# One core, an attention block with memory and an MLP: another hand-over order of the jobs, and the PSUM banks that go with it

## Chip, core and metric

One NeuronCore of a Trainium2 chip runs the whole program. The metric is the device time of one execution in microseconds. The kernel before takes 713.09 us, the median of three runs (712.26 to 713.43).

## What is computed

```python
x = A_x                                   # [1, 2048, 512]
xn = _layernorm(x)
return x + _A_ref(xn, wq, wk, wv, wo, beta) + _B_ref(xn, w1, b1, w2, b2)

def _A_ref(...):                          # 32 heads of 16, 4 segments of 512 tokens
    for s in range(4):
        logits = einsum("bhqd,bhkd->bhqk", qs, ks) * scale + mask
        a_dot = softmax(logits) @ vs
        a_mem = (phi(qs) @ M) / (phi(qs) @ z + 1e-6)
        outs.append(g * a_mem + (1 - g) * a_dot)
        M = M + phi(ks).T @ vs;  z = z + sum(phi(ks))
    return concat(outs) @ wo

def _B_ref(...):                          # 512 -> 1792 -> 512
    y = _layernorm(x)
    return gelu(y @ w1 + b1) @ w2 + b2
```

`phi(t)` is `t + 1` above zero and `exp(t)` below; `g = sigmoid(beta)`.

## The kernel before

Work is cut into **jobs**, a few instructions each. Attention has 16 units: unit i is segment i // 4 and a group of eight heads. The MLP has 16 half blocks: half block j is 256 tokens and half of the 1792 hidden columns. Most products are made of f16 high and low parts, three matmuls for one (`split3`, L465).

The jobs that the prediction speaks of, by the first word of their key, with the lines of their instructions:

- T: projection of queries or keys of a unit, 12 matmuls (L465, `xnT` with `wqs` or `wks`). ACT and DVE take the result out of PSUM (L481 to L495), SP stores it in DRAM (L486 to L488, `qd` or `kd`) and reads it back in another layout (L491, `qst` or `kst`). Scores of the unit can start only after that round trip.
- M: scores for the row maxima (L590, on PE) and the maxima on DVE (L597). R: one transpose (L605) and a second round trip of the maxima (L610, L613).
- S: scores the other way round (L630), exponentials on ACT (L635), masking on POOL (L644). pv and PV: probabilities times values (L659). O: the division (L507 to L513, L689 to L695).
- N, K, Z, Qd, Q: the memory part (L501, L569, L538, L543 to L550).
- V: values (L465). out: the output projection (L783).
- X, Xt, Y, Yt: normalization and transposes of the tokens (L450).
- D: one of the 7 hidden tiles of a half block, 12 matmuls of 256 columns (L465, `yT` with `w1s`), taken out by ACT or DVE (L724, L726). G: gelu (L731). H: the f16 split on POOL and ACT (L738 to L740). e: one of 14 parts of the second MLP product, six matmuls (L764).
- wl, wm, wf, ws: load, square sum, scale and f16 split of the weights, at the start.
- warm: eight matmuls on a tile of ones, whose result nobody reads (L796). There are 14 such jobs.

TensorE works in three **tilings**, which the trace shows as rows*columns of the array: the full array, 128*128 (T, V, D, out, N, transposes, warm); two tiles of 64 rows, on which two matmuls run side by side (M, S, e, Qd; shown as 48\*128, 50\*128 and 64\*128 after the rows in use); and four tiles of 32 columns, 128*32 (pv, K, R).

The order of all 1335 jobs is one string, `ORDER`. Each letter names one of 28 streams, and `plan()` takes the next job of that stream. A job hands its instructions to all engines at once, so the string sets the order on PE, ACT, DVE, POOL and SP, and each engine keeps it. A second string, `BANKS`, gives for every PSUM tile that a job takes (`dense()`) one of eight banks. A matmul that takes a bank waits until the last reader of the bank's previous tile is done.

Of the kernel before, what the change touches and what calls it, by code (L numbers as in the profile page):

```python
# [57 lines left out]
def streams():  # L58
# [43 lines left out]


ORDER = (
    "aacttuttcacutvaatcvucuevaatevaacvccvutbcbwtccvtbvvcwfvwtdcvttxxextxvwyxbchxgxxyxoowxoyxowowvyoyzoyzniiibccyygpz"
    "iiccniipznzyiyfzAnsqpiioiqizzmAqqiwpAzhoAoiiqqzzjpocjiqijjqizjoAjoBAiikskkAkjqiqjqmjjisqjiojiqbiskkkpkibbplafoA"
    "oAjpgjloojqjqjqjlohakkkpkojiqiAajsoijijqjiqjmiAiAifippBkkqqBikipqikoqilBsgaoplahqjjqlqqqjqjoBoijqiajqipamkkkksa"
    "ioojpiqjqiqijqjiaaqjqjsbmqiqBiiBfoikkkbBpkbibpghopoolqqpjqojjjloojiqjqiqilmkpkkkijojiqqqijjqijqiqjqiipkkkpkbiif"
    "mnillnglnnrjjrjqiirpjiqjisqijqikkmkkjijrjjioijioijikkpkkhilmfolomjjbgojqqjpljqjoobsmbkkkkjqqisjqqjijqiqjiqijoiq"
    "iiskkmippqiqpiskaklmiohlfoiqpqaqamqgploooaomjqjqqjqmjqaojpqpsiiqiqoioiqjpqiqiikkkkoapjiqijqijqjpqiqjqsjaqaoihkk"  # L110
    "kkaalmoqjjlbfobqjqjlsqmjgbbqjkkmmkkjqjqmojjjohiojiikkkkipiifplilonnliiiniipmripgnojjmjrjsjorijibkkkpkmiiqjqjqij"
    "qqiijsqiqjohjqiiqpqiipmkpkkskrillfmmlogqqbjjoojqjqjjoomkkpkkiijhooiqjiqjqijqiqpsjiqqjibbpqiqipkkkkliiqaslfoioom"
    "papqqqamgpooasjqqjqjmaoojqjlqjqiqiapqikmkikkiqipoiqjqjaoohijqjaqiqiisopaojiqqjiakmspkkklbopfjqlbqjmjgqjjqqjqlob"
    "bkkkmkmjqjqqiqjqijqjqoimijkpkkkliilfnimiiplgnniipirmoiorponijpjobojjioisjqqjpiiqkkkkiiprijsqsqjiqqjjimqqijrijkk"
    "ipkbsklfloqjqmjglojjqqqjjomsokkkkopjmioiijojqijqipqjqjqiiqqiikppkkkliqlfbbqliqqqimoipmgooojpjqqjojjoomjiikkkpki"
    "qijqijqjqiijqjiqjqiikisqpiskkkqpioqplooplqjjqqjjojjqlopkkkkjqjqqjjojqjoqqpspqkkkkqpqqlqqpqqmpqqqqqqqqqqqmqllqqr"
    "rrr"
)

BANKS = (
    "012345670123456174052316753401627354106237540612375406123754016237516237516237516231756237153672153675213675213"
    "675213765726132567132567132561723516725314607314607314067430167340176340167430167430164301643701643016743021543"
    "021435140235143021542301540123540125340125340152340152403156274031562740351640351640531640513645013465016354016"
    "354016354016354016534016534160543154602731452670315426073154206734215063741253741065370265237065237062537056237"
    "052635270635270652706523706532741534271354274135271435271435271435217406357214035610431054613054613054613054630"
    "546135045061345067123450673152046731520467315204637152046371520463715204637120543670512437065172065210765027106"
    "257106257106257106275062701652704136572043162045731625371627513627153627153627153627513267521376503476547036543"
    "706543765403765403765437403765403765403746052416052461052104621054621056421056241602543176032154760321547603215"  # L130
    "746032157460321576403215764302157642157641572647215762415274627154761245671267456741253607412536401720513674203"
    "764230764230764230764230764203726403752614037512640735124065214502615401256405126405164052164052164051264703512"
    "64351263451263470"
)


# [743 lines left out]
```

## Time and profile before

| | us |
|---|---|
| median of three runs | 713.09 |
| the profiled execution | 712.69 |
| its span, first to last instruction | 711.0 |
| PE busy | 693.3 |
| ACT busy | 535.9 |
| DVE busy | 531.8 |
| POOL busy | 363.7 |

A busy PE in this table is one that has a matmul in flight. A matmul of 512 columns is shown with about 380 ns, though in a row they start 216 ns apart, so the speed of PE has to be read from where groups start, not from their length. In the timeline a row's first number is the start of its group, and the start of the next row says how long the group held PE.

### The profile page before, as it was taken

The page shows a single profiled execution, that of the slowest core. Times are in us where ns is not written, and L with a number is a line of the kernel's source. Part 1 is how long each engine was busy: PE and PEld are TensorE (multiplying, and loading weights), DVE is VectorE, ACT ScalarE, POOL GpSimd, SP SyncE. Part 2 cuts the span into 40 slices and gives each one's busy share as a digit, 9 for nine tenths or more (in the row PEclk, how much of TensorE's full clock was granted, in tenths as well). Part 3 has the DMA queues.
Part 4 walks back from the last instruction along what each step waited for, and adds up shares of the span by engine and source line. Part 5 has one row for each costly group of instructions (what it writes and reads, how often), then busy time and mean ns, then how long its engine had stood idle before and what let it go on. Part 6 is the DMA issues. An engine that isn't in the chain of part 4 may idle for free.

```text
span 711.0 us, 16718 instructions
## 1 busy us (share of the span) xinstructions
PE 693.3 (98%) x6261; PEld 392.6 (55%) x6261; DVE 531.8 (75%) x1665; ACT 535.9 (75%) x934; POOL 363.7 (51%) x548
## 2 busy tenths in 40 slices
PE   7799999999999999999999999999999999999997
PEld 5464556565654565656554656566545545565542
DVE  5889867979684968978686786979688567978243
ACT  6897898868884678586975777687794768778960
POOL 4675758565632354555624446464724455455652
PEclk9999999999999999999999999999999999999999
DMA  9885233232303124131311412340413215031001
GB/s 288 236 247 152 61 71 96 62 90 74 95 4 103 60 70 113 48 96 42 92 43 57 111 47 77 96 115 2 115 24 103 78 20 146 15 93 19 1 17 59
DMA packets 54093, 59.30 MB, mean 83 GB/s; under 512 B 5038, under 2 KB 40892, under 8 KB 54012
## 3 DMA queue, kind: packets, MB, share of 16 engines
q1 hardware_dynamic: 51708, 54.04, 26.5%
q0 software_dynamic: 2304, 4.20, 3.8%
q8 instruction: 49, 0.80, 0.5%
q14 instruction: 32, 0.26, 0.1%
HBM read 41.18 MB, written 17.04 MB: 82 GB/s over the span
## 4 chain that ended last, share of the span: by engine, by line
PE 67%; DVE 12%; ACT 8%; DMA 6%; POOL 4%; issue 3%; SPq 1%; POOLq 0%; DVEq 0%; ACTq 0%
PE ps L465 26%; PE ps L764 14%; PE ps L659 8%; PE ps L783 6%; PE ps L630 4%; PE ps L590 4%; DVE ps L597 4%; ACT pt L635 3%; DMA kd<-hl 2%; PE ps L450 2%; PE ps L538 1%; DVE hl L485 1%; DMA w1s<-in_B_w_dram 1%; DVE mc L597 1%; DMA pt<-in_A_wv_dram 1%
## 5 line engine op out<-in xcount | busy, mean ns | idle before, releaser
L597 DVE CUSTOM_DVE_ANT_0 ps<-ps,mask 128x512 f32<-128x512 f32 (+3 forms) x512 | 235.0, 524 | 24.1 <-PE ps L590 23.2
L635 ACT ACTIVATE pt<-ps,qkcs 128x512 f32<-128x512 f32 (+1 forms) x384 | 206.9, 628 | 20.2 <-PE ps L630 17.7
L764 PE MATMUL ps<-w2s,hT 64*128 64x512 f16 x1344 | 176.2, 376 | 0.3 <-DVE fence L767 0.2
L465 PE MATMUL ps<-yT,w1s 128*128 128x256 f16 x1344 | 161.2, 273 | 2.5 <-DVE phk L495 1.2
L644 POOL TENSOR_SCALAR_AFFINE_SELECT pt<-pt 128x256 f32<-128x256 f32 x256 | 101.6, 419 | 110.1 <-ACT pt L635 109.2
L465 PEld LDWEIGHTS <-w1s 128*128 128x128 f16 x1344 | 127.2, 98 | 37.4 <-issue 16.9
L764 PEld LDWEIGHTS <-hT 64*128 64x128 f16 x1344 | 70.0, 94 | 57.4 <-issue 9.6
L740 POOL TENSOR_TENSOR hT<-hh,hT 128x512 f16<-128x512 f32 x64 | 66.5, 1039 | 66.7 <-ACT hT L739 65.5
L659 PE MATMUL ps<-pt,vt 128*32 128x512 f32 (+3 forms) x1024 | 77.6, 436 | 0.1
L597 DVE DVE_READ_ACCUMULATOR2_ANT mc<- 128x1 f32 x512 | 72.6, 142 | 0.2
L630 PE MATMUL ps<-qst,kst 50*128 50x512 f16 (+3 forms) x512 | 70.6, 298 | 0.1
L590 PE MATMUL ps<-kst,qst 48*128 48x512 f16 (+3 forms) x512 | 67.2, 298 | 0.7 <-DVE hT L726 0.4
L739 ACT ACTIVATE hT<-hh 128x512 f16<-128x512 f32 x64 | 36.7, 574 | 37.4 <-POOL hh L738 37.2
L738 POOL TENSOR_SCALAR hh<-hT,sc 128x512 f32<-128x512 f32 x64 | 42.6, 666 | 38.5 <-ACT hT L731 37.1
L659 PEld LDWEIGHTS ps<-pt,vt 128*32 128x32 f32 x1024 | 30.6, 109 | 42.0 <-issue 31.4
L724 ACT ACTIVATE hT<-ps,b1t,sc 128x256 f32<-128x256 f32 x64 | 36.6, 571 | 17.1 <-PE ps L465 16.6
L465 PE MATMUL ps<-xnT,wqs 128*128 128x512 f16 x192 | 45.0, 384 | 0.4 <-DVE mc L597 0.4
L783 PE MATMUL ps<-wos,oT 128*128 128x512 f16 x192 | 44.0, 380 | 0.9 <-POOL oT L695 0.6
L465 PE MATMUL ps<-xnT,wks 128*128 128x512 f16 x192 | 44.2, 380 | 0.0
L465 PE MATMUL ps<-wvs,xnT 128*128 128x512 f16 x192 | 43.5, 379 | 0.6 <-DVE hT L726 0.3
L726 DVE TENSOR_SCALAR hT<-ps,sc,b1t 128x256 f32<-128x256 f32 x48 | 25.7, 539 | 24.5 <-PE ps L465 24.4
L590 PEld LDWEIGHTS <-qst 48*128 48x128 f16 x512 | 27.1, 94 | 30.7 <-issue 14.8
(217 smaller groups left out, 958.7 us busy)
## 6 DMA issues: line engine op xcount, KB each, us to landing
xt<-in_A_x_dram SPq DMA_DIRECT2D x30, 256.0 KB
kd<-hl SPq DMA_DIRECT2D x48, 128.0 KB
kst<-kd SPq DMA_DIRECT2D x32, 192.0 KB
qd<-hl SPq DMA_DIRECT2D x48, 128.0 KB
qst<-qd SPq DMA_DIRECT2D x32, 192.0 KB
acc<-in_A_x_dram SPq DMA_DIRECT2D x16, 256.0 KB
acc<-in_B_b_dram POOLq DMA_DIRECT2D x16, 256.0 KB, 4.3
out_dram<-acc SPq DMA_DIRECT2D x16, 256.0 KB
```

Source lines behind the costliest of these rows:

```text
L465: T.matmul(p, wsl(ws, k, a), xsl(xs, k, b), start=s0 and i == 0, stop=s1 and i == 3 * n - 1)
L590: T.matmul(p[:, o:o + n], stk[i, 0][r, t, P * qb:P * qb + P], stk[i, 1][r, t, :n], start=True, stop=True)
L597: V.tensor_tensor_reduce(p[:, o:o + n], p[:, o:o + n], mask[:, 512 - n:], 1.0, -3e38, OP.add, OP.max, mc[i][:, 4 * b + t, qb:qb + 1])
L630: T.matmul(p[:, o:o + n], stk[i, 1][r, t, P * kb:P * kb + P], stk[i, 0][r, t, P * kb:], start=True, stop=True)
L635: A.activation(e[:, OFF[kbs[0]]:OFF[kbs[0]] + o], p[:, :o], AF.Exp, scale=qkcs[:, 1, i % NG:i % NG + 1])
L644: G.affine_select(v, v, pattern=[[0, 2], [1, P]], compare_op=OP.is_ge, fill=0.0, base=0, channel_multiplier=-1)
L659: T.matmul(p[32 * c:32 * c + 32, P * kb:], vt[s, kb][:, 4 * g + c, 16 * odd:16 * odd + 32], pt[i, 2 * c + odd][:, OFF[kb]:OFF[kb] + LEN[kb ...
L738: G.tensor_scalar(t, hz[:, z, :], col(SHH + j % 2), 0.0, op0=OP.mult, op1=OP.add)
L739: A.activation(hT[:, z, 0, :], t, AF.Copy)
L740: G.tensor_tensor(hT[:, z, 1, :], t, hT[:, z, 0, :], op=OP.subtract)
L764: T.matmul(pes[j][a], hTs[fh][r, fi, u, P * a:P * a + P], w2s[r, fo, v, :], start=n == 0 and m == 0, stop=fi == FH - 1 and m == 2, skip_gr ...
L783: T.matmul(p, o[:, u, P * b:P * b + P], wos[:, g, v, :], start=i == 0, stop=i == 3 * NG - 1)
```

## The change

The strings `ORDER` and `BANKS` are replaced by others of the same length, `ORDER` by the same letters in another order. No line of code is changed, and every engine runs the same computing instructions; only the waits between them are placed anew.

```diff
 ORDER = (
-    "aacttuttcacutvaatcvucuevaatevaacvccvutbcbwtccvtbvvcwfvwtdcvttxxextxvwyxbchxgxxyxoowxoyxowowvyoyzoyzniiibccyygpz"
+    "aacuccteauacvcacccttttutaatvaebvcbcuvvvttwdvabwccuvftvvvxctbvtwxwwxgeyxcyxxwwxxghoxoyoxccxoozyiiiozoiiyypzzpnii"
...
 BANKS = (
-    "012345670123456174052316753401627354106237540612375406123754016237516237516237516231756237153672153675213675213"
+    "012345670123456170324561732504617253046172530461725306172453061742061742016742016742017642017642016741260471264"
...
```

The following places show it. First PE, where the first MLP product of half block 9 (L465 with `w1s`, a full-array job) stands among scores of unit 9 (L630) and the memory update (L569). Each L465 row with another number of `ps` is one job D; rows that repeat are left out. Before:

```order
L630 LDWEIGHTS kst1_92
L630 MATMUL ps5_6279<-qst1_90,kst1_92 128x256
L630 MATMUL ps2_6280<-qst1_90,kst1_92 128x256
L465 LDWEIGHTS w1s_103
L465 MATMUL ps7_6287<-yT_5160,w1s_103 128x256
L465 MATMUL ps0_6301<-yT_5160,w1s_103 128x256
L569 MATMUL ps4_6315<-vt0_85,pkn_5973 32x48 x4
```

Now:

```order
L630 LDWEIGHTS kst1_92
L630 MATMUL ps2_6266<-qst1_90,kst1_92 128x384
L630 MATMUL ps1_6267<-qst1_90,kst1_92 128x384
L465 LDWEIGHTS w1s_103
L465 MATMUL ps7_6282<-yT_5099,w1s_103 128x256
L465 MATMUL ps0_6296<-yT_5099,w1s_103 128x256
L465 MATMUL ps5_6310<-yT_5099,w1s_103 128x256
L450 MATMUL ps3_6325<-ident_74,xt_5302 128x128 x4
L450 MATMUL ps6_6332<-ident_74,xt_5304 128x128 x4
```

Three jobs D and two transposes, all full-array jobs, stand in a row where two stood.

Second, PE again, where the scores of unit 14 begin (L590 with `kst0` and `qst0`), just behind the last job D of half block 13. Before:

```order
L465 LDWEIGHTS w1s_103
L465 MATMUL ps6_8732<-yT_7591,w1s_103 128x256
L630 LDWEIGHTS kst1_92
L630 MATMUL ps0_8752<-qst1_90,kst1_92 128x512
L630 MATMUL ps7_8753<-qst1_90,kst1_92 128x512
L590 LDWEIGHTS qst0_89
L590 MATMUL ps4_8764<-kst0_91,qst0_89 128x512
L590 MATMUL ps1_8765<-kst0_91,qst0_89 128x512
```

Now:

```order
L465 LDWEIGHTS w1s_103
L465 MATMUL ps0_8731<-yT_7560,w1s_103 128x256
L796 LDWEIGHTS ones_79
L796 MATMUL ps7_8745<-ones_79 128x256
L590 LDWEIGHTS qst0_89
L590 MATMUL ps5_8760<-kst0_91,qst0_89 128x512
L590 MATMUL ps2_8761<-kst0_91,qst0_89 128x512
```

One of the 14 warm jobs (L796) now stands directly ahead of these scores. Another stands between the sixth job D of half block 2 and the transpose N of unit 2; the other twelve are at the start, where all 14 were.

Third, DVE in the start-up, where the weights are split (L377), the first hidden tiles come out of PSUM (L726) and the first row maxima are taken (L597, shown as ISA here). Before:

```order
L726 TENSOR_SCALAR hT0_112<-ps7_597,sc_106,b1t_114 128x256
L377 SCALAR_TENSOR_TENSOR wvs_101<-pt_290,sc_106,wvs_101 128x512 x2
L377 SCALAR_TENSOR_TENSOR wqs_99<-pt_216,qksc_107,wqs_99 128x512
L726 TENSOR_SCALAR hT0_112<-ps5_634,sc_106,b1t_114 128x256
L377 SCALAR_TENSOR_TENSOR w2s_104<-w2s_104,sc_106 128x512
L597 ISA ps0_684,mc_683<-ps0_684,mask_81 128x512
```

Now:

```order
L367 SCALAR_TENSOR_TENSOR sc_106<-sc_106 128x1
L377 SCALAR_TENSOR_TENSOR w1s_103<-w1s_103,sc_106 128x512
L726 TENSOR_SCALAR hT0_112<-ps1_609,sc_106,b1t_114 128x256
L597 ISA ps2_642,mc_641<-ps2_642,mask_81 128x512
L597 ISA mc_641 128x1
L597 ISA ps5_643,mc_641<-ps5_643,mask_81 128x512
```

The row maxima of unit 0 now come ahead of the third hidden tile that DVE takes out and of the first split of `w2s`.

More of the change, by code (lines that the diff above doesn't have):

```diff
@@ L104 @@
 ORDER = (
-    "aacttuttcacutvaatcvucuevaatevaacvccvutbcbwtccvtbvvcwfvwtdcvttxxextxvwyxbchxgxxyxoowxoyxowowvyoyzoyzniiibccyygpz"
[L106 to L114, printed above, removed]
@@ L115 @@
-    "ipkbsklfloqjqmjglojjqqqjjomsokkkkopjmioiijojqijqipqjqjqiiqqiikppkkkliqlfbbqliqqqimoipmgooojpjqqjojjoomjiikkkpki"
-    "qijqijqjqiijqjiqjqiikisqpiskkkqpioqplooplqjjqqjjojjqlopkkkkjqjqqjjojqjoqqpspqkkkkqpqqlqqpqqmpqqqqqqqqqqqmqllqqr"
+    "aacuccteauacvcacccttttutaatvaebvcbcuvvvttwdvabwccuvftvvvxctbvtwxwwxgeyxcyxxwwxxghoxoyoxccxoozyiiiozoiiyypzzpnii"
+    "ibnizysyfznqiqiczvczpoizyynoiwooiqipiqqmAzzqAjspisojojjqijqqjiscAhiAikkzbkkisijqjiqjqjqijoAbibjqpkAkkkfpoAojAAg"
+    "jjlopomljjjloothkkiiAmkAkpqqjiiqjqijqjqjjaafoikkkkppiAiBsghpBaqiiiqqqiqqBpBoiaalpooioijqjlojajaoajjqolmiiaabpkk"
@@ new lines @@
+    "kkijqqBsibqijqjqijqqijiqjqiqispmkkkkiBbbpfooBBjqjlgoopjlqjqjjlqmokkkkjiiopijojiqjqijqjqiqiqipikkkklilgnniimhfln"
+    "irrrppqsiipjqqjqjqijqijqiqipnijikkkkmssiijojijobjjimrijkkkpkhllfobjmjgoooljjqjqjobbkmmkkkiqjqjimsqjqqiijqjqijqi"
+    "qipaikkhiqppiqkkliilofoiopaqamgpooaaomoqjqqjqjqjqjjqmqiqiilpkkkksiiqqpaiqqijpohaoajioosjqjpqqiijqqijqipaaosikkb"
+    "mskkllofjbqqmjgoblbqjqjqjqqqjqmmkkkkijioojbiiohjijojjomipikkkkliiiolfnniimplnimgrojjjrjjjnspkkkmkipijrhpsiqijqi"
+    "qiqjqijqqijiqqqijiqqimppkkkkirllfomjlgoopojbqjjqjmooobbjqqiipkkkkmpiiqjqiqijqqjmsijqiqjiqqijqiiapskkkkhisplaoal"
@@ L117 @@
+    "fmqqjplgpooooajjjooaqjjqiqiiqqqiipkkpkkaiqijqiqqpjjaooajiqjiqijqikkmkmkiaahbosmplplofqjmpqbjgloojqjjqjombbkkkkj"
+    "qqiqqssiijqqjqijjqqijqqibkkmkkmlpiliifnnoimiiplogonoimpnrrijiojsiprobjjjsorijipkkkkqjiqqjiqjqijqqijiqjqiqipmkkk"
+    "kpillfoompqgqjpsqqjmjloooojjjotmiipkkkkiqjqijqjqijqqijqiiqjkskkkpiipfbbplqqqiqqiolimgpmlooojjqojjjoomjiipskkkki"
+    "jjiqiqjqijqijqijqqiiiqqiqsspkkpkipklpooolqjjjqqqjjjloopkkkkjjqojqjqqjjoqqsqqqkkkkqppplpqqmqqqqqqpqqqqqqmqqlqqlr"
     "rrr"
@@ L128 @@
[L128 to L132, printed above, removed]
@@ L133 @@
-    "64351263451263470"
+    "012345670123456170324561732504617253046172530461725306172453061742061742016742016742017642017642016741260471264"
+    "701624701624710624174016253704621357042163570462315047623076420732067432067342067342607342607342607326402673402"
+    "673426073145260731452604752064756240756247056247056274506275460275436012745316207465231076451047561407561407561"
+    "047561407561407450671450671456071423560472135046732510467235102346750124375064132075641325641325462153462513461"
@@ new lines @@
+    "235463152463156231564231561423075621453017453017457301457301574301537041570354170365240326452603452063450623540"
+    "264305264305172463052174065321740652317406532174065321746053217460532174605321746053172456301724310724037120432"
+    "701430217430217403742170342170536421750432650436520463520345620354632054605324605234634052176340512763540123541"
+    "023541023514023514023514025314205423105243510243571605276152076152076512076751627051267056172430516724305617243"
+    "056172403561274506371420563714205637201456340516430513604513605413605416305463107524631075246731052463172461372"
@@ L134 @@
+    "436172436173624173624173624173621347620153476250134672503410637250637250632753206753206752360752360745123640751"
+    "23654123654123654"
 )
```

4 lines of the change are left out of this document (removed).

## Prediction

> **What bounds the kernel now.** I read the stages first, because an average over the span mixes two regimes. The view of stages gives, for each stretch, its length and then the busy time of PE, PEld, DVE, ACT and POOL, the granted TensorE clock, and the DMA share.
>
> ```profile
> 0.00:20.00 20.00, 15.53 (x111) 12.00 (x112) 12.70 (x36) 13.02 (x30) 8.87 (x22) 1.00 0.98 288
> 20.00:60.00 40.00, 35.77 (x232) 21.77 (x231) 34.23 (x110) 36.17 (x61) 25.50 (x25) 0.96 0.78 221
> 60.00:100.00 40.00, 38.15 (x404) 21.35 (x402) 34.94 (x135) 34.89 (x64) 26.00 (x38) 1.00 0.29 79
> 100.00:200.00 100.00, 99.67 (x958) 59.70 (x957) 79.73 (x251) 83.35 (x151) 59.22 (x87) 1.00 0.32 84
> 400.00:500.00 100.00, 100.00 (x984) 60.56 (x983) 83.03 (x267) 78.12 (x133) 50.81 (x79) 1.00 0.25 63
> sum 560.00, PE 558.41 PEld 315.95 DVE 433.69 ACT 425.89 POOL 278.38; mean PE 93.07 PEld 52.66 DVE 72.28 ACT 70.98 POOL 46.40
> ```
>
> In the first 20 us DMA is full. From 20 to 100 us ACT and DVE are busy some 87 to 90% of the time with weight splits and evictions, and PE, with the warm jobs counted, is not yet what everything waits for. From 100 to 660 us (the sum row) PE has a matmul in flight for 558.41 of 560 us, while ACT and DVE are busy 426 and 434 us, some 77%. So the first 100 us are a start-up set by the loads and by ACT and DVE, and the rest is set by PE.
>
> A busy PE need not be PE at its pace, so I went to the timeline of PE and read the distance from one group's start to the next.
>
> ```profile
> 547.22 1.47 PE L465 MATMUL ps<-yT,w1s 128*128 128x256 f16 x12
> 548.53 0.27 PE L605 MATMUL ps<-ident,mc 128*32 128x128 f32 x1
> 548.64 1.47 PE L465 MATMUL ps<-yT,w1s 128*128 128x256 f16 x12
> 549.95 2.75 PE L783 MATMUL ps<-wos,oT 128*128 128x512 f16 x12
> ...
> 424.73 2.79 PE L465 MATMUL ps<-yT,w1s 128*128 128x256 f16 x24
> 427.45 0.28 PE L630 MATMUL ps<-qst,kst 50*128 50x256 f16 x2
> ...
> 358.45 1.48 PE L465 MATMUL ps<-yT,w1s 128*128 128x256 f16 x12
> 359.87 0.28 PE L630 MATMUL ps<-qst,kst 50*128 50x256 f16 x2
> ...
> 366.05 0.39 PE L590 MATMUL ps<-kst,qst 48*128 48x512 f16 x2
> 366.37 1.49 PE L465 MATMUL ps<-yT,w1s 128*128 128x256 f16 x12
> ...
> 428.22 0.38 PE L630 MATMUL ps<-qst,kst 50*128 50x512 f16 x2
> 428.44 0.81 PE L764 MATMUL ps<-w2s,hT 64*128 64x512 f16 x6
> ```
>
> Twelve L465 matmuls hold PE for 1.31 us when a full-array job follows (548.64 to 549.95), and for 1.42 us when a 64-row job follows (358.45 to 359.87): 0.11 us more. Twenty-four hold it 2.72 us (424.73 to 427.45) against twice 1.31: 0.10 us more. In the other direction a pair of 64-row matmuls holds PE 0.22 us before another 64-row job (428.22 to 428.44) and 0.32 us before a full-array job (366.05 to 366.37): again 0.10 us. **A change between full rows and 64 rows costs 0.10 us**, and nothing hides it where PE is the bound. A change of columns alone does not show it: before L605 in 128\*32 the twelve matmuls take the same 1.31 us (547.22 to 548.53).
>
> With such start distances (216 ns for 512 columns, 109 for 256, half of it for one of a pair) the matmuls of the stage from 100 to 660 us come to some 523 us, and its changes of rows to about 20 us. The other 14 us or so are small waits that no row of the wait view shows as large:
>
> ```profile
> PE ps L465 <- DVE phk L495: 1.2, 1, 1.2
> PE ps L465 <- DVE mc L597: 0.6, 2, 0.4
> PE ps L465 <- DVE hT L726: 0.5, 2, 0.3
> ```
>
> So the old order is tight. Another order has little to win beyond the changes of tiling, and it can lose by making waits.
>
> **The change part by part.** No instruction is added or removed; what changes is the order on the engines and the bank of each tile.
>
> *Tiling changes.* Counted over the 5523 matmuls of PE in program order, neighbours of different tiling fall from 284 to 240; of these, changes between full and 64 rows fall from 242 to 202 and changes of columns alone stay near 40. Split at the point where PE has done 100 us of its own work (warm jobs not counted), the row changes go from 50 to 43 ahead of it and from 192 to 159 behind it. Ahead of it ACT and DVE set the pace, and I count nothing. Behind it 33 changes go: 33 x 0.10 = **-3.3 us**. At the low end all 40 count, -4.0; at the high end the time comes back as waits, 0.
>
> The Trainium skill, "TensorEngine Tiling (Array Packing)", section "Tiling Modes", says that changing the tiling mode, and not just the tile, drains TensorE. The row changes agree with their 0.10 us. The column changes do not: 1.31 us with and without one. By the rule every change would count, 38 of which fall in the stage set by PE, and the term would be -3.8 us in place of -3.3.
>
> *Warm jobs.* All fourteen stood in the start-up, where PE had time. Two now stand inside. One job of eight is priced by this row, whose 24 matmuls in a row take 2.79 us, 0.11 each:
>
> ```profile
> 24.76 2.79 PE L796 MATMUL ps<-ones 128*128 128x256 f16 x24
> ```
>
> That is 0.9 us a job. The one at unit 2 lies at about 94 us of PE's work, where ACT and DVE are still nearly full, and I take 0 for it. The one ahead of unit 14's scores fills the time in which those scores wait for their queries (next part): without it the distance would be 10.0 us and PE would wait about 0.8 us. So it costs **+0.1 us**. Bounds: 0 and 1.8 us.
>
> *The round trip of queries and keys.* The chain of waits shows it whole once, for unit 8:
>
> ```profile
> 347.54 0.53 ACT hl L481
> 348.07 0.59 ACT phq L484
> 348.68 0.69 DVE hl L485
> 349.40 4.37 DMA qd<-hl
> 353.79 0.31 SPq L491
> 354.15 3.94 DMA qst<-qd
> 358.13 0.39 PE ps L590
> ```
>
> PE left the last matmul of that projection at 347.27 (next row of its timeline, below), and the scores' second row tile starts at 358.13, so the trip takes about 10.8 us.
>
> ```profile
> 344.67 2.76 PE L465 MATMUL ps<-xnT,wqs 128*128 128x512 f16 x12
> 347.27 1.04 PE L450 MATMUL ps<-ident,xt 128*128 128x128 f32 x8
> ```
>
> I added PE's own work, changes included, between the end of each query projection and the first score of its unit. From unit 3 on the short ones were 10.2, 10.2, 10.6, 10.7 and 10.7 us (units 3, 8, 12, 14, 15). In the new order they are 10.5, 10.2, 10.2, 10.8, 10.9 and 10.1 (units 3, 4, 8, 12, 14, 15). What is missing to 10.8 adds to 1.6 us before and 2.2 us now: **+0.6 us**. If the trip is 1 us longer than the one row shows, both sums grow nearly alike, so the bounds are 0 and +1.5.
>
> *PSUM banks.* For each bank I compared PE's work between the last matmul of one tile and the first of the next. For L630's tiles, which ACT reads, a tenth of the distances were under 1.16 us and now under 1.51; for L590's, which DVE reads, a tenth were under 1.40 and now under 1.55; the medians go from 2.36 to 2.38 and from 2.89 to 2.61. Neither way: **0**, with 3 us either side, a fifth of the 14 us of small waits.
>
> *Start-up.* Pricing every ACT and DVE instruction by its line's mean and adding them up in program order gives how much work stands ahead of the same point of PE's own work:
>
> ```profile
> L597 DVE CUSTOM_DVE_ANT_0 ps<-ps,mask 128x512 f32<-128x512 f32 (+3 forms) x512 | 235.0, 524 | 24.1 <-PE ps L590 23.2
> L635 ACT ACTIVATE pt<-ps,qkcs 128x512 f32<-128x512 f32 (+1 forms) x384 | 206.9, 628 | 20.2 <-PE ps L630 17.7
> ```
>
> At 32 us of PE's work ACT has 48.6 us ahead before and 48.4 now, DVE 45.2 and 48.7; at 40 us ACT 56.9 and 54.4, DVE 55.9 and 57.3; at 80 us ACT 95.1 and 94.0, DVE 89.0 and 89.2. The fuller engine is the same within 1.1 us at each point, and the difference is gone at 80 us: **0**, bounds -1 and +3.5 (DVE's surplus at 32 us).
>
> The Trainium skill, "TensorE: Matmul & The Clock Gate", Part 1, speaks against moving warm jobs out of the start: after an idle window of about 3.4 us the clock falls to half. This trace shows a granted clock of 0.96 from 20 to 60 us; how the new gaps fall no row can tell. The sum does not use it.
>
> *The end.* The same jobs follow the last exponentials of unit 15 in both orders, and DVE's last divisions stand behind the same part e: 0.
>
> The sum, from the profiled execution's span: 711.0 - 3.3 + 0.1 + 0.6 = 708.4 us. The median of the three runs lies 2.1 us above that span, so I predict 710.5 us, 0.36% less. A measurement of this kernel can tell about 0.2%, 1.4 us, from no change.
>
> **Rivals.**
>
> *The start-up ends later.* DVE takes the maxima of unit 0 ahead of a split of `w2s` that the first parts e need. Counted with the warm jobs, at 44 us on PE's account, DVE has 45.2 us of work ahead before and 50.6 now, 5.4 us more. For it: DVE is busy 34 of 40 us there. Against it: ACT has as much ahead in both, and by 80 us the sums meet. If PE gets its operands 5.4 us later and never makes it up, the span is 708.4 + 5.4 = 713.8, the time 715.9 us. It makes the kernel slower from a delay of 4.0 us on (2.6 us of the forecast's gain and 1.4 us).
>
> *Nothing comes of it.* PE reaches its next operands 3.3 us earlier, and they are not there: ACT and DVE have their work at the old pace. For it: ACT is at 83% and DVE at 80% from 100 to 200 us, and the 14 us of small waits show that operands are often just in time. Against it: both have over 20 us spare in each 100 us. The time would be 713.09 + 0.7 = 713.8 us.
>
> *More than the changes of tiling.* If the order and the banks also take a third of the 14 us of small waits, 4.7 us more go: 705.8 us. For it: the shortest bank distances grew. Against it: the medians of L590 fell.
>
> **How the numbers follow.** Forecast 0.45 (its own range 708 to 712, a ninth of its chance within 0.2% of before), more than that 0.18, nothing 0.14, a later start-up 0.23. The range holds 8 in 10: from the third rival, 705.5, to just above the first, 716.5. Faster by over 0.2% (under 711.7): 0.18 from the third, 0.40 of the forecast's 0.45, and 0.03 of the rest, together 0.61. Within 0.2%: 0.16. Slower: 0.23.
>
> **What would show it.** In the profile after: groups of twelve L465 matmuls still at 1.31 and 1.42 us, with 40 fewer of the longer kind; the stage set by PE shorter by about 3 us between the same jobs; ACT's and DVE's busy sums unchanged; PE waiting for the second `qst` load at the first L590 of units 4, 8 and 15. The first job e of half block 0 should come within 2 us of where it was; if it is 4 us late, the first rival holds. If the changes are fewer and the waits of PE more by as much, the second does. The forecast is wrong if the span lies outside 706 to 710 us.

## The result, and the profile after

The changed kernel takes 715.50 us, the median of 7 runs (714.37 to 716.90), beside 712.67 us (712.18 to 714.72, 7 runs) for the kernel before on the same chip. The ratio is 1.0036, with a 95% interval of 1.0021 to 1.0051: slower by 0.36%, where 0.36% faster was forecast. The profiled execution took 714.92 us with a span of 713.1, against 711.0 before.

The view of stages of the changed kernel, with the columns of the one shown before:

```profile
0.00:20.00 20.00, 13.87 (x98) 10.59 (x99) 12.62 (x48) 13.21 (x30) 8.68 (x23) 0.98 0.98 286
20.00:60.00 40.00, 34.00 (x216) 19.97 (x216) 31.34 (x101) 32.50 (x56) 21.92 (x22) 0.92 0.79 226
60.00:100.00 40.00, 38.16 (x357) 22.12 (x359) 35.31 (x128) 33.20 (x64) 26.22 (x37) 1.00 0.33 88
100.00:200.00 100.00, 99.83 (x1010) 60.33 (x1012) 79.83 (x251) 89.46 (x160) 62.12 (x94) 1.00 0.28 74
400.00:500.00 100.00, 99.05 (x970) 61.42 (x969) 83.32 (x276) 76.80 (x132) 52.34 (x80) 1.00 0.25 64
```

Two stages differ. From 20 to 60 us ACT is busy 32.50 us in place of 36.17 and DVE 31.34 in place of 34.23: both wait for something. From 400 to 500 us PE is busy 99.05 us, where it had a matmul in flight all the time. A stage by the clock holds different work in the two orders, though, so I also compare at equal work: for each matmul I add up the start distances of all matmuls ahead of it (216 ns for 512 columns and so on, warm jobs and changes of tiling not counted), and read at what time the trace reaches 40, 100, 380 and 460 us of this sum, which ends at 633 us. A line runs from PE's first matmul to its last, so it adds up to some 5 us less than the span. The first two lines of the table are the result; the rest are the experiments below. Changes of tiling between full and 64 rows (row changes) are in brackets.

| us spent from .. to .. of PE's own work | 0 to 40 | 40 to 100 | 100 to 380 | 380 to 460 | 460 to end |
|---|---|---|---|---|---|
| before | 70.2 | 68.5 | 297.0 (104) | 84.6 (27) | 185.7 (61) |
| changed | 72.9 | 68.0 | 293.9 (91) | 87.8 (19) | 185.7 (49) |
| a_par2_late | 71.3 | 68.1 | 293.9 | 87.8 | 185.7 |
| a_warm_fill | 70.8 | 68.1 | 293.9 | 87.7 | 185.6 |
| a_fix | 71.0 | 68.0 | 294.7 | 87.7 | 185.6 |
| a_local | 71.3 | 68.0 | 294.5 | 87.4 | 185.5 |
| before_start | 70.3 | 71.9 | 294.2 | 87.8 | 185.5 |
| after_start | 73.4 | 76.7 | 296.9 | 84.7 | 185.7 |
| b_par2_early | 71.3 | 68.9 | 296.8 | 84.6 | 185.6 |
| b_start2 | 70.7 | 68.2 | 297.1 | 85.1 | 185.6 |
| mix380 | 70.3 | 68.1 | 295.4 | 88.0 | 186.0 |
| mix748 | 71.1 | 68.0 | 295.7 | 84.8 | 185.7 |
| b375_after | 71.0 | 69.2 | 297.1 | 87.8 | 185.5 |
| b380_after | 70.5 | 68.4 | 297.2 | 98.2 | 185.5 |
| a_ungather | 70.1 | 68.0 | 303.3 (113) | 88.7 (25) | 187.4 (59) |
| a_ungather2 | 70.0 | 68.0 | 301.7 (125) | 87.8 (23) | 185.6 (49) |

So the new order loses 2.2 us up to 100 us of work (72.9 + 68.0 against 70.2 + 68.5), wins 3.1 up to 380, loses 3.2 up to 460, and is even behind. That makes +2.3 us, and the spans differ by 2.1.

**The start.** PE's timeline of the changed kernel:

```profile
16.49 0.20 PE L808 MATMUL ps<-ident,mhl 14*128 14x14 f32 x1 [1.93 <-DMA mhl<-in_B_b_dram]
...
18.51 0.38 PE L465 MATMUL ps<-xnT,wks 128*128 128x512 f16 x1
20.58 4.85 PE L465 MATMUL ps<-xnT,wks 128*128 128x512 f16 x11 [1.69 <-DVE xnT L454]
```

L808 is job par2 (the bias `b1` turned round; behind it DVE works out the decay, L809 to L815). It now stands ahead of the first key projection, and PE waits 1.93 us for its load. The first matmul of the projection, in its own row, starts at 18.51; the others wait until 20.58 for DVE, which has par2's block and the scales in its queue. Then eleven matmuls take 4.65 us (20.58 to 25.23, where the next group starts), not 2.4. Two rows of the view of stages, the changed kernel's and then that of before, say why; the number ahead of the last two is the granted clock:

```profile
20.00:25.00 5.00, 4.42 (x11) 1.62 (x11) 1.78 (x3) 1.47 (x4) 2.35 (x3) 0.50 1.12 326
```

```profile
20.00:25.00 5.00, 3.04 (x21) 1.75 (x20) 2.83 (x8) 3.94 (x8) 2.95 (x4) 1.00 1.06 293
```

The projection ran at half clock. That was not this execution alone: the mean granted clock of the seven runs is 0.992 to 0.995, and 0.994 to 1.000 in the 23 runs of the kernel before that were measured beside a_par2_late. And what is queued behind the projection on ACT waits with it. ACT's timeline, changed:

```profile
19.21 1.05 ACT L313 ACTIVATE wvs<-pt 128x1024 bf16<-128x1024 f32 x1
...
20.86 0.62 ACT L380 ACTIVATE wks<-wks 128x512 f16<-128x512 f32 x1
25.47 0.60 ACT L481 ACTIVATE hl<-ps 128x512 f16<-128x512 f32 x1 [4.00 <-PE ps L465]
...
28.28 1.69 ACT L313 ACTIVATE w1s<-w1s 128x1792 bf16<-128x1792 f32 x1
```

Before:

```profile
22.20 1.04 ACT L313 ACTIVATE wvs<-pt 128x1024 bf16<-128x1024 f32 x1
...
23.24 0.58 ACT L481 ACTIVATE hl<-ps 128x512 f16<-128x512 f32 x1
...
25.42 1.69 ACT L313 ACTIVATE w1s<-w1s 128x1792 bf16<-128x1792 f32 x1
```

In the old order a square sum of `wvs` (L313) stood between the split of `wks` and the eviction (L481), so ACT came to the eviction at 23.24, after the projection had ended (21.4), and did not wait. In the new order that square sum comes 3 us earlier, ACT reaches the eviction early and waits 4.00 us, and the square sum of `w1s`, on which the first hidden tiles rest, starts at 28.28 in place of 25.42.

**The body.** Waits of PE from 430 to 525 us, in us, times, and the longest:

```profile
PE ps L764 <- DVE hT L726: 0.5, 1, 0.5
PE ps L630 <- DVE phq L495: 0.3, 1, 0.3
PE ps L590 <- DVE mc L597: 0.3, 1, 0.3
PE ps L630 <- ACT hT L724: 0.2, 1, 0.2
PE ps L764 <- DVE hl L485: 0.2, 1, 0.2
PE ps L630 <- DVE mc L597: 0.2, 1, 0.2
```

For the kernel before this view lists none between 430 and 525 us. All six are PSUM banks: PE wants to write a tile, and ACT or DVE has not yet read the tile that was in the bank. `BANKS` bears it out: at each of the six, the engine and line named are those that read the bank's previous tile. One of the places, all engines:

```profile
444.42 0.14 DVE L767 COPY fence<-ps 1x1 f32<-1x1 f32 x1
444.49 1.31 DVE L527 TENSOR_TENSOR zr<-bd,mst 64x64 f32<-64x64 f32 x4
...
445.83 0.70 DVE L597 CUSTOM_DVE_ANT_0 ps<-ps,mask 128x512 f32<-128x512 f32 x1
446.56 0.08 DVE L597 DVE_READ_ACCUMULATOR2_ANT mc<- 128x1 f32 x1
446.56 0.69 DVE L597 CUSTOM_DVE_ANT_0 ps<-ps,mask 128x512 f32<-128x512 f32 x1
446.69 0.40 PE L630 MATMUL ps<-qst,kst 50*128 50x384 f16 x4 [0.18 <-DVE mc L597]
...
447.36 0.28 PE L590 MATMUL ps<-kst,qst 48*128 48x256 f16 x2 [0.27 <-DVE mc L597]
```

DVE takes job Z of unit 10 (four instructions, 1.31 us) ahead of row maxima, and PE stands twice for the banks of these maxima. The other three places, PE alone:

```profile
469.43 0.39 PE L630 MATMUL ps<-qst,kst 50*128 50x512 f16 x2 [0.23 <-ACT hT L724]
...
503.33 0.37 PE L764 MATMUL ps<-w2s,hT 64*128 64x512 f16 x1 [0.47 <-DVE hT L726]
503.93 0.80 PE L764 MATMUL ps<-w2s,hT 64*128 64x512 f16 x5 [0.22 <-DVE hl L485]
...
511.69 0.40 PE L630 MATMUL ps<-qst,kst 50*128 50x384 f16 x4 [0.33 <-DVE phq L495]
```

Here a 64-row job (S or e) follows on gathered D and T jobs, and takes a bank that one of these filled (D.10.2 at 469.43, D.11.3 and T.12.1 at 503, T.12.0 at 511.69); a projection T alone hands ACT two instructions and DVE three. A bracket shows only the time in which PE had nothing in flight. Measured by the start distances, the four places cost 0.75, 0.7, 1.0 and 0.4 us, 2.9 in all.

### The profile page after: what moved, and what is told of

The parts are those of the page before. It is cut to its first block, busy times and chain, and to the rows that moved or that the text cites. A ratio compares the mean times of both kernels' runs of the same rounds, so it can differ in the third digit from the quotient of the medians.

```text
span 713.1 us, 16730 instructions
## 1 busy us (share of the span) xinstructions
PE 690.2 (97%) x6261; PEld 399.8 (56%) x6261; DVE 532.8 (75%) x1665; ACT 535.8 (75%) x934; POOL 363.3 (51%) x548
## 4 chain that ended last, share of the span: by engine, by line
PE 69%; ACT 11%; DVE 9%; POOL 5%; issue 3%; SPq 1%; DMA 1%; POOLq 0%; DVEq 0%; ACTq 0%
PE ps L465 28%; PE ps L764 15%; PE ps L659 8%; PE ps L783 6%; PE ps L630 4%; PE ps L590 4%; DVE ps L597 3%; ACT pt L635 3%; PE ps L450 1%; PE ps L538 1%; ACT w1s L313 1%; ACT hT L739 1%; POOL hT L740 1%; SPq L254 1%; DMA mhl<-in_B_b_dram 1%
## 5 line engine op out<-in xcount | busy, mean ns | idle before, releaser
L597 DVE CUSTOM_DVE_ANT_0 ps<-ps,mask 128x512 f32<-128x512 f32 (+3 forms) x512 | 234.5, 525 | 19.1 <-PE ps L590 16.8
L465 PE MATMUL ps<-yT,w1s 128*128 128x256 f16 x1344 | 159.6, 273 | 2.9 <-POOL w1s L381 1.5
L465 PEld LDWEIGHTS <-w1s 128*128 128x128 f16 x1344 | 128.1, 98 | 33.9 <-issue 11.2
L764 PEld LDWEIGHTS <-hT 64*128 64x128 f16 x1344 | 75.5, 94 | 59.7 <-issue 13.7
L740 POOL TENSOR_TENSOR hT<-hh,hT 128x512 f16<-128x512 f32 x64 | 66.8, 1044 | 68.4 <-ACT hT L739 66.9
L659 PE MATMUL ps<-pt,vt 128*32 128x512 f32 (+3 forms) x1024 | 76.9, 436 | 0.1
L597 DVE DVE_READ_ACCUMULATOR2_ANT mc<- 128x1 f32 x512 | 72.7, 142 | 0.1
L630 PE MATMUL ps<-qst,kst 50*128 50x512 f16 (+3 forms) x512 | 67.8, 297 | 1.4 <-ACT hT L724 0.4
L590 PE MATMUL ps<-kst,qst 48*128 48x512 f16 (+3 forms) x512 | 67.3, 297 | 1.4 <-DVE hT L726 1.0
L659 PEld LDWEIGHTS ps<-pt,vt 128*32 128x32 f32 x1024 | 30.1, 109 | 42.5 <-issue 32.1
L465 PE MATMUL ps<-xnT,wks 128*128 128x512 f16 x192 | 46.6, 394 | 1.7 <-DVE xnT L454 1.7
L689 POOL TENSOR_TENSOR nN<-nN,oT 128x512 f32<-128x512 f32 x16 | 20.5, 1282 | 51.1 <-DVE oT L513 51.1
L465 PE MATMUL ps<-xnT,wqs 128*128 128x512 f16 x192 | 44.2, 380 | 0.0
L465 PE MATMUL ps<-wvs,xnT 128*128 128x512 f16 x192 | 43.6, 379 | 0.4 <-DVE mc L597 0.4
L590 PEld LDWEIGHTS <-qst 48*128 48x128 f16 x512 | 28.5, 94 | 27.0 <-issue 11.9
```

Of the source, the lines that this page charges most:

```text
L465: T.matmul(p, wsl(ws, k, a), xsl(xs, k, b), start=s0 and i == 0, stop=s1 and i == 3 * n - 1)
L590: T.matmul(p[:, o:o + n], stk[i, 0][r, t, P * qb:P * qb + P], stk[i, 1][r, t, :n], start=True, stop=True)
L597: V.tensor_tensor_reduce(p[:, o:o + n], p[:, o:o + n], mask[:, 512 - n:], 1.0, -3e38, OP.add, OP.max, mc[i][:, 4 * b + t, qb:qb + 1])
L630: T.matmul(p[:, o:o + n], stk[i, 1][r, t, P * kb:P * kb + P], stk[i, 0][r, t, P * kb:], start=True, stop=True)
L659: T.matmul(p[32 * c:32 * c + 32, P * kb:], vt[s, kb][:, 4 * g + c, 16 * odd:16 * odd + 32], pt[i, 2 * c + odd][:, OFF[kb]:OFF[kb] + LEN[kb ...
L740: G.tensor_tensor(hT[:, z, 1, :], t, hT[:, z, 0, :], op=OP.subtract)
```

## Experiments

Orders are written as lists of jobs. "New" is the changed kernel's order, "old" that of before; each bank goes with its job. Every ratio is to the kernel before on the same chip, with its 95% interval; a time is a median. A trace is of one execution, and that can be faster than the median.

### The start: par2 and the warm jobs

a_par2_late takes the new order and moves par2:

```diff
 wm.v.0
-par2
 wf.QK
...
 wf.v
+par2
 wm.1a.1
```

> The changed order with one job moved: the transposition of b1 (L808, with its DVE block L809 to L815) goes back behind the scale of the value weights, instead of standing ahead of the last token transpose and the first key projection. Theory 1 (the start-up is late because this job waits for the load of b1, 1.9 us on PE, and holds 1.5 us of DVE work ahead of the last xnT split, after which the first projection runs at half clock): the first projection ends about 3.5 us earlier, the start-up's 2.7 us go, time 712.5 to 713.5 us against 715.5 for the changed order. Theory 2 (ACT's weight splits set the start-up, and the projection only shifts within it): less than 1 us, 714.5 to 715.5. Theory 3 (the waits behind 430 us are what costs): no change, 715.5.

Measured: 714.47 us (12 runs), ratio 1.0026 (1.0016 to 1.0037), 1.0 us less than the changed kernel, or 0.7 by the ratios, whose intervals overlap. That is between the ranges of the first two theories. Its trace, of the fastest of the 12 runs, is 1.6 us ahead of the changed kernel's at 40 us of work and 1.5 at the end.

a_warm_fill takes the new order and moves the two late warm jobs into the start, where PE stood still:

```diff
+warm
 par2
...
+warm
 T.0.1
...
 D.2.5
-warm
 N.2
...
 D.13.6
-warm
 Z.14
```

> The changed order with its two late warm jobs moved to the start, one ahead of the transposition of b1 and one ahead of the first key projection, where PE stands idle. If the half clock of that projection comes from the idle time, it runs in 2.6 us instead of 4.7, and the two jobs no longer cost anything in the body: time 712 to 713. If the clock falls anyway: only the body's part, 0.9 us for the job at unit 2 and up to 0.9 for the one ahead of unit 14's scores, 714 to 714.7. If both jobs were fillers in the body: 715.5 less nothing.

Measured: 714.01 us (12 runs), ratio 1.0017 (1.0007 to 1.0027), 1.5 us less than the changed kernel, or 1.4 by the ratios. The median lies in the range of the second case, in which the clock falls anyway. In the trace, though, which is of the fastest of the 12 runs (712.70 us), the projection ran at full clock:

```profile
18.81 1.04 PE L796 MATMUL ps<-ones 128*128 128x256 f16 x8
19.68 0.38 PE L465 MATMUL ps<-xnT,wks 128*128 128x512 f16 x1
20.87 2.53 PE L465 MATMUL ps<-xnT,wks 128*128 128x512 f16 x11 [0.82 <-DVE xnT L454]
```

The trace is 2.1 us ahead of the changed kernel's at 40 us of work and 2.2 at the end, so in this execution the start's gain is kept. Without the warm job ahead of unit 14's scores the last stage is 0.1 us shorter.

a_fix does both, with the second warm job ahead of wf.1a:

```diff
-par2
 wf.QK
...
+warm
 T.0.1
...
 wf.v
+par2
...
+warm
 wf.1a
...
-warm
 N.2
...
-warm
 Z.14
```

> The changed kernel with three jobs moved, all in the start-up: par2 from ahead of wf.QK to behind wf.v, one of the two late warm jobs to ahead of the first key projection, the other to ahead of wf.1a. Theory (the loss of the start-up is par2 in front of the first key projection, and the half clock in which that projection then runs): both losses go together, PE is within 0.7 us of the kernel before at 40 us of its own work, the stage from 100 us of work to the end lasts as in the changed kernel, and the time is 712.4 to 713.6 us, no more than 0.1% from before. Rival (each of the two edits already took the same 1.5 us, and the rest of the start-up's loss lies in the order of the weights): 714.0 to 714.5 us, with PE still 1.5 us late at 40 us of work.

Measured: 713.53 us (11 runs), ratio 1.0008 (1.0000 to 1.0017). Of the 0.36% some 0.28 are gone, 2.0 us: the start-up's loss, and no rest of it that could be told. By the ratios the two edits alone gave 0.7 and 1.4 us, about the same sum, but neither is known well enough to tell whether they overlap. The clock still fell: in the trace of a_fix the projection again takes 3.7 us (19.89 to 23.60) at a granted clock of 0.50 from 18.8 to 22.1 us, with a warm job directly ahead of it.

b_par2_early turns it round, par2 moved forward in the old order:

```diff
+par2
 wf.QK
...
 warm.10
-par2
```

> The kernel before with one job moved, par2 from behind warm.10 to ahead of wf.QK, as in the changed kernel. Theory (par2 ahead of the first key projection costs 1.5 us, by DVE's block of L809 to L815 ahead of the tokens and the wait for the load of mhl): 714 to 714.8 us, and the first key projection ends 1 to 2.5 us later. Rival (it costs only in the new order, where fewer warm jobs stand in front): 712.5 to 713.3 us.

Measured: 713.48 us (12 runs), ratio 1.0002 (0.9993 to 1.0010). The theory's number missed: the profiled execution was 1.1 us late at 40 us of work, the runs show almost nothing. The projection ended 0.8 us later (22.2 us in place of 21.4). So par2 in front does not cost 1.5 us by itself. Moving the warm job that stands ahead of the projection as well gives b_start2:

```diff
+par2
 wf.QK
-warm.9
 Yt.0.0.0
...
 T.0.1
+warm.9
...
 warm.10
-par2
```

> The kernel before with two jobs moved, which puts the front of the changed kernel's start into the old order: par2 ahead of wf.QK, and warm.9, the eight matmuls directly ahead of the last transposes and the first key projection, behind that projection. Theory (par2 ahead and no warm job there, so that the projection comes late and at a low clock): the first key projection ends 2 us or more later than in the kernel before, the loss stays to the end, and the time is 714.3 to 715.5 us, ratio 1.002 to 1.004. Rival (the clock falls somewhere in the start in nearly every run whatever stands there, and in the old order the projection is followed by a wait that takes up the delay): 712.5 to 713.6 us.

Measured: 713.41 us (11 runs) beside 712.35 for the kernel before on the same chip, ratio 1.0013 (1.0004 to 1.0022). That is the rival's range in microseconds; the pair costs about half of what its absence saved in the new order. ACT, in its timeline, shows no wait at the eviction:

```profile
24.16 0.58 ACT L481 ACTIVATE hl<-ps 128x512 f16<-128x512 f32 x1
```

But what the theory speaks of did not come about here: the projection ended at 21.6 us, 0.2 us later than before and not 2, and the granted clock was 1.00 from 20 to 30 us. So whether the square sum of `wvs` ahead of L481 would cover a late projection was not tested.

What the runs show is that the start's loss goes when par2 and the two warm jobs are moved back in the new order (a_fix), and that moving par2 and one warm job the other way costs about half as much in the old order. By which path they cost it, the clock, DVE's queue or ACT's, was read from the traces, and none of these was tried alone. For ACT's queue speaks that its first square sum of `w1s` starts at 25.42 us before, 26.34 in b_start2, 26.61 in a_fix and 28.28 in the changed kernel, and 40 us of work are reached in the same order, at 70.2, 70.7, 71.0 and 72.9 us.

### The first splices

before_start and after_start exchange the start at 56 us of PE's work:

```diff
-ORDER = new
+before_start = old[:188] + (new without these jobs)
+after_start = new[:186] + (old without these jobs)
```

> The first 188 jobs as in the order before, all others in the changed order; the banks follow the jobs, 8 of 1127 differ. Theory 1 (the start-up costs 2.7 us): the lead of the order before at 24 to 70 us of PE's own work is gone, and the body keeps what it has: time 712.0 to 713.0, ratio to before 0.999 to 1.000. Theory 3 (the waits in the body make the kernel slower, and the start would have been made up): 715 to 716, ratio 1.003.

> The other half: the changed order up to the same point, then all others in the order before; 14 banks differ. Theory 1: 715.0 to 716.0, ratio 1.003 to 1.004. Theory 3: as before, 712.7, ratio 1.000.

Measured: 716.3 us, ratio 1.0048 (1.0033 to 1.0063), and 724.73 us, ratio 1.0167 (1.0152 to 1.0182). Both say nothing of the start: at the seam, jobs of one order met others that in their own order had come earlier, and PE stood for 3 us and for some 8 more (the column 40 to 100 has 71.9 and 76.7 us in place of 68). A part of that is clock: the granted clock was 0.50 from 93.7 to 97.0 us and from 98.4 to 101.7 us, behind waits of PE of 1.59 and 2.06 us. From 100 us of work on each runs like the order its body comes from. The start has to be judged by the moves above, and a seam has to be chosen.

### Are changes of rows on the path?

a_ungather swaps 19 pairs in a_fix to bring 38 changes of rows back, for example:

```diff
-D.4.1
...
 S.3.0.0
+D.4.1
...
-M.5.11
...
 out.0.3
+M.5.11
```

> The order of a_fix with 19 pairs of neighbouring jobs swapped behind 100 us of PE's work, each at a border between full rows and 64 rows, so that 38 changes of rows come back (159 to 197) and nothing else moves by more than one job. Theory (a change of rows costs 0.10 us on the path also where the body waits elsewhere): 3.8 us more than a_fix, 3 to 4.6. Rival (the saving is hidden, PE just waits less where it loses time at a change): less than 1.5 us more than a_fix.

Measured: 724.14 us, ratio 1.0154 (1.0141 to 1.0167), 10.6 us more than a_fix. That is far over 0.10 each, and its trace has new steps of 1.4, 1.9 and 1.0 us, among them transposes R that now follow their last score directly and wait for DVE. The step of 1.9 us is followed by a fall of the clock, which adds over 1 us more (the twelve L465 matmuls in it hold PE 2.66 us):

```profile
323.20:326.50 3.30, 3.30 (x18) 1.91 (x19) 1.19 (x5) 1.32 (x5) 1.06 (x2) 0.50 0.01 2
```

Behind 100 us of work the trace takes 11.4 us more than a_fix's (the table). The new steps sum to some 6.5 us of it, and some 4.9 are left for the 38 changes, 0.13 each. a_ungather2 uses other swaps, after which nothing comes closer to what it needs by more than 0.25 us of PE's work:

> Again the order of a_fix with 19 jobs moved past a neighbour so that 38 changes of rows come back (159 to 197 behind 100 us of PE's own work), but other ones: all between 100 and 430 us of work, each such that no tile comes closer than before to what it needs, nor a bank to its last use, by more than 0.25 us. Theory (a change of rows costs 0.10 us on the path, and what a_ungather lost beyond that were waits made by the moves): 3.8 us over a_fix, 716.8 to 718.2 us, with no new wait over 0.5 us in the trace. Rival (waits hide the changes, and a_ungather lost by its moves alone): less than 1.5 us over a_fix, under 715 us.

Measured: 721.01 us (4 runs), ratio 1.0118 (1.0100 to 1.0137). The expected number missed again: the stage from 100 to 440 us of work is 7.1 us longer than in a_fix, and its trace has steps of 0.4 to 0.7 us with 2.7 to 3.2 us in all, for instance

```profile
PE ps L590 <- DVE acc L771: 0.6, 2, 0.3
PE ps L590 <- ACT nD L668: 0.6, 1, 0.6
```

What is left is 3.9 to 4.4 us, 0.10 to 0.12 per change. How much of a step is a wait of its own was judged from the traces, so the price per change is an estimate; the rival, that waits hide the changes, would leave less than 1.5 us and is out in both runs. Behind the last swap the two orders take the same time to 0.1 us: a delay in the middle is not made up.

### Where the body loses

mix380 and b380_after join the orders at 380 us of PE's work:

```diff
-ORDER = new
+mix380 = a_fix[:830] + (old without these jobs)
+b380_after = old[:835] + (new without these jobs)
```

> The order of a_fix up to the point where PE has done 380 us of its own work (job 829 of 1335), and behind it what is left in the order and with the banks of the kernel before; the two sets of jobs differ there by eight. Theory (gathering pays 0.10 us per change also in the middle, and the loss lies in particular places of the new order between 380 us of work and the end): the gain of the first part stays, 712.8 less about 3 us, 709 to 710.5 us, ratio 0.995 to 0.997. Rival (ACT and DVE set the pace over hundreds of us, so that time saved on PE comes back as waits wherever the order comes from): the waits come back behind the seam, 712.3 to 713.5 us.

> The converse: the order of the kernel before up to 380 us of PE's own work (job 835), behind it what is left in the order of the changed kernel. Theory (the places of the new order behind 380 us lose about 5 us in waits and win 2 us in changes of rows): 712.8 plus about 3 us, 715 to 716.5 us. Rival (those waits came only because PE was ahead of ACT and DVE): they don't come here, and the 20 fewer changes behind 380 us of work make it 710.3 to 711.5 us.

Measured: 714.77 us, ratio 1.0027 (1.0017 to 1.0036), and 727.67 us, ratio 1.0200 (1.0182 to 1.0219). Neither is in the range of either theory: both seams were bad again. In mix380 most of the loss is one place at the seam, where probabilities times values wait for POOL's mask:

```profile
435.94 1.20 PE L659 MATMUL ps<-pt,vt 128*32 128x256 f32 x14 [1.55 <-POOL pt L644]
```

In b380_after PE waits 5.55 us at 470.33 for DVE (L544), and the granted clock is 0.50 from 467.7 to 474.4 us. Then I looked for seams at which no job comes nearer to what it needs than in both orders:

```diff
-ORDER = new
+mix748 = a_fix[:748] + (old without these jobs)
+b375_after = old[:829] + (new without these jobs)
```

> The order of a_fix up to job 748 (337 us of PE's own work), behind it what is left in the order and with the banks of the kernel before. At this seam no score, no transfer and no division comes closer to what it needs than in both orders, and one bank does by 1.3 us. Theory (the changes of rows saved up to there, 120 against 132 at 320 us of work, stay saved): 1.4 to 2 us under the kernel before, 710.8 to 711.6 us, ratio 0.997 to 0.998. Rival (the pace of ACT and DVE takes it back behind the seam): 712.5 to 713.5 us.

> The order of the kernel before up to job 829 (375 us of PE's own work), behind it what is left in the order and with the banks of the changed kernel; at this seam nothing comes closer to what it needs than in both orders. Theory (the new order behind 380 us of work loses some 5 us in waits of its own against 2 us of saved changes): 712.8 plus 3 us, 715.3 to 716.5 us. Rival (those waits arise only because PE runs ahead of ACT and DVE there): 710.3 to 711.5 us.

b375_after: 716.3 us (5 runs), ratio 1.0044 (1.0030 to 1.0058), in the theory's range. The new order's waits come at the same jobs, though PE arrives there 2.5 us later and from the old order:

```profile
449.16 0.40 PE L630 MATMUL ps<-qst,kst 50*128 50x384 f16 x4 [0.18 <-DVE mc L597]
449.83 0.28 PE L590 MATMUL ps<-kst,qst 48*128 48x256 f16 x2 [0.27 <-DVE mc L597]
```

In every run with the new order and a good seam, the stage from 380 to 460 takes 87.4 to 87.8 us, and with the old one 84.6 to 85.1. The loss belongs to the order of that stage, not to PE's being early.

mix748: 714.01 us (12 runs, 712.55 to 718.30), ratio 1.0017 (1.0002 to 1.0032), which misses the theory's 710.8 to 711.6. Its profiled execution was the fastest of the 12 (712.55 us). There the stage from 100 us of work to the end takes 566.2 us against 567.3 before, in spite of 1.0 us of a wait for a bank at the seam. Counted by the same jobs, it is 0.9 us ahead of the kernel before just behind the seam (M.9.0 starts at 394.29 in place of 395.23) and 0.7 us ahead at the last part e, 300 us later. So in this execution next to nothing was taken back. The runs spread over 5.8 us, though, and their median is 0.9 us over the old order's on that chip (713.10); what the slower of them lost, and where, no trace shows. No version came out faster than the kernel before.

a_local moves two jobs Z in a_fix:

```diff
-Z.6
 A.5.1
...
 e.4.6
+Z.6
...
-Z.10
 A.9.0
...
 M.10.9
+Z.10
```

> The order of a_fix with two jobs of the memory part moved behind their neighbours: Z.6 (four DVE instructions, L527) from ahead of part e.4.4 to behind e.4.6, whose last instruction on DVE is the fence (L767) that e.4.7 waits for, and Z.10 from ahead of M.10.6 to behind M.10.9. Theory (the body gives its saving back as single waits, each where the new order puts a burst of DVE work ahead of a tile that PE needs at once): the steps at 275 us (0.8) and at 446 us (0.75) are gone, nothing comes in their place, and the time is 1.3 to 2 us under that of a_fix, 711.6 to 712.3 us. Rival (ACT and DVE set the pace over long stretches, so a wait that is removed comes back a little later): 713.2 us or more.

Measured: 713.16 us (12 runs), ratio 1.0006 (0.9994 to 1.0018), the rival's number. The two waits went, but others came:

```profile
276.58 0.72 PE L630 MATMUL ps<-qst,kst 50*128 50x384 f16 x3 [1.10 <-DVE mc L597]
```

```profile
451.87 0.28 PE L605 MATMUL ps<-ident,mc 128*32 128x128 f32 x1 [0.42 <-DVE mc L597]
```

DVE's 1.3 us has to stand somewhere, and near it maxima or a transpose come late. Moving it took 0.3 us off the stage from 380 to 460.

## Why the prediction was wrong

*Changes of tiling, -3.3 us.* The term held. Groups of twelve L465 matmuls still take 1.31 or 1.41 us in the new order, the 33 changes are gone, and 38 put back cost 0.10 to 0.13 us each on the path. One part of its count was off by 0.2 us: changes between the full array and four tiles of 32 columns, which it took as free, do cost (last section).

*PSUM banks, 0.* This is the step that failed in the body. "For each bank I compared PE's work between the last matmul of one tile and the first of the next", and the medians and tenths of these distances were alike; but such a distance says how long PE is away, not what stands ahead of the reader on ACT and DVE. I worked the distance out from `ORDER`, `BANKS` and the start distances for the six waits above: it is 1.73, 1.94, 3.38, 4.31, 1.72 and 3.59 us, in order of time. All six are over the prediction's shortest tenth (1.51 and 1.55 us), and three are over its medians (2.38 and 2.61). So the measure could not have shown these places. Measured by stage: 13 changes fewer and 3.1 us less from 100 to 380 us of work, so 1.8 us fewer waits; 8 fewer and 3.2 us more up to 460, so 4.0 us more waits; 12 fewer and no less time behind, so 1.2 us more, the warm job included. Together +3.4 us. This is what remains of each stage's time, and not a sum of waits seen: of the 4.0 us the four places explain 2.9. The prediction's 3 us either side nearly held it.

*Start-up, 0.* The second step that failed: +2.2 us. "The fuller engine is the same within 1.1 us at each point" compares sums of work. It missed that ACT and DVE would stand still: 4.00 us for ACT at one eviction, with the weights' square sums queued behind. Its high end, +3.5, held it, but that was DVE's surplus of work, and not this wait.

*Warm jobs, +0.1.* Right for the one at unit 14 (0.1 us by a_warm_fill). The one at unit 2 cost 0.8 us at 80 us of work, made up by 100. Taking warm jobs out of the start did cost there. The rule of the Trainium skill, "TensorE: Matmul & The Clock Gate", Part 1, which the sum did not use, spoke against it, and the granted clock of 0.50 from 20 to 25 us agrees in sign. No single wait of PE ahead of that fall was longer than 1.93 us.

*Round trip, +0.6.* Not seen: no wait for `qst` at units 4, 8 or 15 in the changed kernel. In a_fix one of 0.45 us shows at unit 8.

*The rivals.* A later start-up came, but not by its mechanism: the first part e starts at 64.3 us, and at 64.1 before.

```profile
L764 PE MATMUL ps<-w2s,hT x138: 372/376/387, 64.1 to 137.2; 64*128 64x512 f16 x138
```

```profile
L764 PE MATMUL ps<-w2s,hT x126: 373/376/387, 64.3 to 139.1; 64*128 64x512 f16 x126
```

"Nothing comes of it" gave the right sum for the body, again for another reason: the waits are not the old pace of ACT and DVE, which would have come back in mix748 too. They are places that this order makes: in b375_after they come at the same jobs. The sum by what was measured is 711.0 - 3.3 + 3.4 + 2.2 = 713.3 us, and the span was 713.1; as 3.4 is a remainder, the sum had to close.

What stays open: a_fix, a_local and the old order cannot be told apart, and why the gathered jobs leave more waits from 380 to 460 than elsewhere was read at four places, and only one of these (Z) tried, which brought no gain that could be told.

## What to carry to other kernels

A saving on the bounding engine is kept only if the new order makes no new waits, and in a tight order the waits weigh as much: here 33 changes of tiling were worth 3.3 us, and the waits of the order that saved them took 3.4. Before one trusts such a saving, look, at each tile that PE writes, at what its bank's last reader has queued ahead of it on its own engine; and in a start-up look for an engine that will stand at an instruction in its queue, not for the sum of its work. To test two orders against each other, splice them where no job comes nearer to what it needs: bad seams here cost 2 to 13 us and hid everything else.

## What the hardware did that was not expected

*The clock in the start.* In every trace here but one the granted clock falls to 0.50 in the start-up, for about 3.4 us, for twice that, or for 3.4 us twice. Windows set on such falls, for the changed kernel, the kernel before and a_local (0.50 throughout; 1.00 just ahead and behind):

```profile
19.30:26.00 6.70, 5.42 (x15) 2.21 (x15) 2.45 (x9) 2.70 (x7) 2.61 (x3) 0.50 1.12 332
```

```profile
29.70:33.00 3.30, 3.30 (x13) 2.25 (x14) 3.02 (x13) 2.47 (x4) 1.73 (x2) 0.50 0.17 60
```

```profile
11.50:14.80 3.30, 3.30 (x16) 2.48 (x15) 2.81 (x9) 2.32 (x5) 2.86 (x10) 0.50 1.08 333
```

The same instructions do not always meet it at the same place. Of six profiles with a_fix's start, three (a_ungather, a_ungather2, mix380) have one fall, at 33 us, and reach 40 us of work at 70.0 to 70.3 us. The other three (a_fix, a_local, mix748) have two, the first at 11 or 19 us and the second at 39, and reach it at 71.0 to 71.3. So one profile does not price a start to better than 1.3 us. The one trace without a fall is b_par2_early, with a clock of 1.00 from 10 to 45 us and waits of PE of 1.87, 2.67 and 1.79 us in it, so a wait of that length does not bring the fall by itself. Between 50 us and PE's last matmul only the four traces named above show a fall, each at or behind a wait of 1.59 us or more that a swap or a seam had made.

*Changes of columns.* The prediction took a change of columns alone to be free, from one row ahead of L605. The new order shows others, with L569 and L659:

```profile
156.44 1.48 PE L465 MATMUL ps<-yT,w1s 128*128 128x256 f16 x12
157.85 0.55 PE L569 MATMUL ps<-vt,pkn 128*32 128x48 f32 x32
...
332.31 2.36 PE L659 MATMUL ps<-pt,vt 128*32 128x512 f32 x32
334.61 0.61 PE L465 MATMUL ps<-yT,w1s 128*128 128x256 f16 x4
...
437.07 2.36 PE L659 MATMUL ps<-pt,vt 128*32 128x512 f32 x32
439.25 0.52 PE L569 MATMUL ps<-vt,pkn 128*32 128x48 f32 x32
...
581.24 2.36 PE L659 MATMUL ps<-pt,vt 128*32 128x512 f32 x32
583.53 0.29 PE L605 MATMUL ps<-ident,mc 128*32 128x128 f32 x1
```

Ahead of L569 the twelve L465 matmuls hold PE 1.41 us, as ahead of a 64-row job, so going from 128\*128 to 128\*32 costs 0.10 us there. The way back costs as much: the 32 matmuls of L659 hold PE 2.18 us ahead of L569, which has their tiling, and 2.30 ahead of L465. Ahead of L605 it is 2.29. So L605, though it is shown as 128\*32, behaves like a full-array job on both sides, and its row says nothing of a change of columns. In the kernel the matmuls of L569 and L659 name a tile position, and the transpose of L605 does not. The prediction's sentence "The column changes do not" was thus read from a place where the tiling seems not to have changed. With L605 counted among the full-array jobs, the changes between these and the jobs in 32 columns go from 17 to 19 behind 100 us of work. That takes 0.2 us off the term: -3.1 in place of -3.3.
